# Loads of w3t units held three to ten units ahead of use, and queued behind the queries, in an attention and MoE kernel

## The chip, the core and the metric

The kernel runs on one core of a Trainium2 chip. Five engines matter: TensorE (PE, with its weight loads PEld), VectorE (DVE), ScalarE (ACT), GpSimd (POOL), and SyncE (SP), which here issues nearly all DMAs. Each engine works through its own list of instructions in a fixed order. The metric is device time in microseconds (us), the median of three runs.

## The reference

Three stages in float32, each fed by the one before. The weights are float64 in memory, q, k and v float32.

```python
def _attn_ref(q, k, v, g_q, g_k):            # (4, 12, 448, 64)
    q_n, k_n = rmsnorm(q, g_q), rmsnorm(k, g_k)
    scores = scale * np.matmul(q_n, k_n.transpose(0, 1, 3, 2))
    scores = scores - np.max(scores, axis=-1, keepdims=True)
    attn = np.exp(scores)
    attn = attn / (np.sum(attn, axis=-1, keepdims=True) + 1e-09)
    return np.matmul(attn, v)

def _moe_ref(x, w_in, w_out):                # 1792 x 768, d_ff 2048
    r = np.maximum(x @ w_in, 0.0)
    return (r * r) @ w_out

def _moe2_ref(x, w1, w2, w3, w_out):         # d_ff 1024
    return ((x @ w1) * (x @ w2) @ w3) @ w_out
```

## The kernel before

The four batches of 448 rows are worked one after the other. The 48 heads (batch b has the heads 12b to 12b + 11) run through a loop over `h`; beside the heads of one batch PE works on the dense layers ("fill") of the batch before. Beside the heads 0 to 12 there is no such batch yet, so the fill is a product of weights alone: `gen_w3o` multiplies w3 with the last w_out, 384 matmuls of 384 columns in 8 row blocks. Beside the heads 12 to 23 the fill is the two MoEs of batch 0 (`gen_moe(0)`), and so on. Below, batch 0 is the stretch of the heads 0 to 11 and batch 1 that of the heads 12 to 23.

**Units.** All weights come in pieces of 128 rows, numbered in the order of use. Units 0 to 31 are for `gen_w3o`: 0 and 5 are the two units of w3t's first row block, 1 to 4 and 6 to 17 are the last w_out, and 18 to 31 are two units of w3t for each of the row blocks 1 to 7. U0 = 32 is the first unit of w_in; units 32 to 119 are the weights of batch 0's MoEs, all of them float64 in memory. A float64 unit goes through these steps: a load into one of four buffers `raw64` (L319, on SP), Prelu on the high words (L333, ACT), the low words (L337 on ACT or L339 on POOL), a join into one of seven buffers `raw` (L346, DVE), a store of the float32 form for the later batches (L354, SP), a rounded high part (L144 `hl<-raw`, ACT) and the rest (L150 `hl<-raw,hl`, DVE or POOL). PE multiplies the parts in three matmuls (L411 to L413).

**A head.** Queries are loaded as `qt` (two buffers, L818) by `load_head`, called three heads ahead, and prepared by `head_prep` (L920 and L925). PE makes scores (L956, L957), DVE takes their negative maximum (L967) and scales it (L969), ACT takes the exponential (L991) into `p`, PE turns it (L1038, `pt`), ACT and DVE split it (`ptr`, `pte`), and PE multiplies with v (L1084, `kv`); DVE sums the two halves (L1092, `xf`). Norms are made for groups of four heads: a square (L862), a sum (L863), and a root by L832 to L839, with Ln and Exp on ACT (L837, L838). Scores have two PSUM banks, so a score waits for an exponential two scores back.

**What sets the order.** The code is traced in the order of the loop, and a scheduler then gives each engine its fixed list: it takes what it holds to be ready first, with the earlier traced one ahead, and it knows how many buffers there are. A load therefore stands early on SP when a `raw64` buffer is free, and its conversion steps stand early on ACT, DVE and POOL. `use(u)` is called by the fill for each unit, and it calls `advance(u)`: that traces the split of units up to u + 2 (u + 4 from U0 on), the joins up to two and the loads up to five (`LOAD64_AHEAD`) beyond that. `tc.issue_after(x)` orders what is traced under it behind instruction x on x's engine. It orders the issue alone; nothing waits until x is done.

Of the kernel before, what the change touches and what calls it, by code (L numbers as in the profile page):

```python
# [1 line left out]

# [9 lines left out]
U32 = mybir.dt.uint32  # L12
# [18 lines left out]
def attention_moe_kernel(  # L31
# [15 lines left out]
    nc = tc.nc  # L47
# [13 lines left out]
    NIC = w3t.shape[0] // 2  # L61
# [201 lines left out]
    def is64(i):  # L263
        return units[i][0].dtype != F32
# [46 lines left out]
    def load_next():  # L311
        i = pos["load"]
        src = units[i][0]
        while sum_of.get(i, -1) >= pos["sum"]:
            next(sums_left, None)
        n = src.shape[-1]
        if is64(i):
            t = t3.tile([128, 512, 2], U32, name="raw64", tag="raw64", bufs=4)
            nc.sync.dma_start(out=t[:, :n, :], in_=src.bitcast(U32).rearrange("p (n t) -> p n t", t=2))  # L319
        else:  # L320
            t = rawp.tile([128, 512], F32, name="raw", tag="raw")
            last["load"] = nc.sync.dma_start(out=t[:, :n], in_=src).ins
        raws[i] = t
        pos["load"] += 1
# [5 lines left out]
    def words(i):  # L330
        t, n = raws[i], units[i][0].shape[-1]
        hi = t[:, :n, 1].bitcast(F32)
        nc.scalar.activation(out=hi, in_=hi, func=AF.Prelu, scale=2.0**-112, alpha=-(2.0**32))  # L333
        low = t.rearrange("p n t -> p (n t)").bitcast(U16).rearrange("p (n t) -> p n t", t=4)[:, :n, 1]
        low_eng = LOW_ENG[i >= U0]
        if low_eng[i % len(low_eng)] == "a":
            nc.scalar.activation(out=t[:, :n, 0], in_=low, func=AF.Copy, scale=2.0**-13, bias=2.0**-14 - 0.5)  # L337
        else:
            nc.gpsimd.tensor_scalar(  # L339
                out=t[:, :n, 0], in0=low, scalar1=2.0**-13, scalar2=2.0**-14 - 0.5, op0=ALU.mult, op1=ALU.add  # L340
            )

    def join(i):
        t, n = raws[i], units[i][0].shape[-1]
        f = raws[i] = rawp.tile([128, 512], F32, name="raw", tag="raw")
        nc.vector.scalar_tensor_tensor(  # L346
            out=f[:, :n].bitcast(U32), in0=t[:, :n, 1], scalar=3, in1=t[:, :n, 0],
            op0=ALU.logical_shift_left, op1=ALU.bitwise_or,
        )
# [33 lines left out]
    def upto(what, i, step):  # L383
        while pos[what] <= min(i, NU - 1):
            step(pos[what])
            pos[what] += 1

    def advance(u):
        while pos["lo"] <= min(u + SPLIT_AHEAD + (2 if u >= U0 else 0), NU - 1):
            i = pos["lo"]  # L390
            for k in range(pos["load"], min(i + LOAD64_AHEAD, NU - 1) + 1):
                if is64(k):
                    load_next()
                elif k <= i + LOAD32_AHEAD and (k <= pos["join"] or not is64(k - 1)):
                    load_next()
                else:
                    break
            upto("store", min(i + JOIN_AHEAD, pos["join"]) - 1, lambda k: is64(k) and store(k))
            upto("word", i + WORD_AHEAD, lambda k: is64(k) and words(k))
            upto("join", i + JOIN_AHEAD, lambda k: is64(k) and join(k))  # L400
            upto("hi", i + HI_AHEAD, split_hi)
            upto("lo", i, split_lo)

    def use(u):
# [408 lines left out]
    def load_head(h):  # L813
        if not (0 <= h < NH):
            return
        b, hh = divmod(h, H)
        t = t2.tile([128, S], F32, name="qt", tag="qt")
        nc.sync.dma_start(out=t, in_=q_t[b, hh])  # L818
        qts[h] = t

    def load_v(h):
# [460 lines left out]
```

## Time and profile before

| | us |
|---|---|
| median of 3 runs | 1159.13 (1157.38 to 1160.3) |
| the profiled execution | 1156.4 |
| its span | 1154.6 |
| PE busy in the span | 1119.4 (97%) |
| DVE busy | 793.3 (69%) |
| ACT busy | 777.1 (67%) |
| POOL busy | 606.5 (53%) |

Busy shares over the span hide stages, so a table of stretches is read beside them: where PE is not full, what else is. A timeline then lists one engine's instructions with start and length; the bracket behind one is the idle time before it and the instruction that ended that. A group line sums instructions of one line and shape. PE's granted clock is a share of full speed, where 0.50 is 1.2 GHz and 1.00 is 2.4 GHz.

### The profile page before, as it was taken

To read this page: it belongs to the slowest core of one execution; us is meant where nothing else is said; L and a number is where in the kernel's file an instruction comes from. 1 tells how busy PE (TensorE), PEld (TensorE's weight loads), DVE (VectorE), ACT (ScalarE), POOL (GpSimd) and SP (SyncE) were. 2 spreads that over 40 slices of the span, in tenths; PEclk is the share of its full clock that TensorE was granted. 3 is DMA by queue.
4 is the path that set the end of the run, shared out by engine and by line. 5 is a ranking of instruction groups with operands and counts; after the bars stand their busy time and mean duration, and the time that the engine had idled before them with its cause. 6 is when DMAs were issued, how large, how long until landed. Compare 5 with 4: busy or idle time off the path is not lost.

```text
span 1154.6 us, 18788 instructions
## 1 busy us (share of the span) xinstructions
PE 1119.4 (97%) x5958; PEld 1015.1 (88%) x5958; DVE 793.3 (69%) x1363; ACT 777.1 (67%) x1768; POOL 606.5 (53%) x609
## 2 busy tenths in 40 slices
PE   7789999999999999999999999999999999999998
PEld 4678888988989899989999899999999899999997
DVE  7899889978988854564674755664544315887886
ACT  6888978978878866767776666776764445433352
POOL 3376433544435455956876775684855853011131
PEclk9899999999999999999999999999999999999999
DMA  7867758878988863575655657665546764243423
GB/s 250 268 194 227 221 156 262 309 273 282 323 274 273 299 197 128 166 220 164 221 178 163 207 184 244 187 200 165 183 155 205 224 191 122 72 134 104 130 84 122
DMA packets 130899, 229.74 MB, mean 199 GB/s; under 512 B 17472, under 2 KB 84544, under 8 KB 130800
## 3 DMA queue, kind: packets, MB, share of 16 engines
q1 hardware_dynamic: 129072, 225.79, 61.3%
q10 hardware_dynamic: 1728, 2.75, 0.7%
q8 instruction: 47, 0.77, 0.3%
q14 instruction: 52, 0.43, 0.1%
HBM read 162.53 MB, written 37.05 MB: 173 GB/s over the span
## 4 chain that ended last, share of the span: by engine, by line
PE 67%; ACT 10%; DVE 8%; DMA 8%; issue 3%; SPq 1%; POOL 1%; DVEq 0%; ACTq 0%; POOLq 0%
PE mm L411 16%; PE mm L412 16%; PE mm L413 16%; PE kv L1084 3%; PE pt L1038 3%; PE sc L956 2%; PE sc L957 2%; ACT p L991 2%; DMA raw<-w_in 2%; ACT raw L333 1%; DMA raw<-wo 1%; DVE nb L967 1%; DVE raw L346 1%; ACT hl L144 1%; DMA qn<-q_nat 1%
## 5 line engine op out<-in xcount | busy, mean ns | idle before, releaser
L150 POOL TENSOR_TENSOR hl<-raw,hl 128x384 fp32r<-128x384 f32 (+1 forms) x286 | 332.2, 1168 | 283.3 <-ACT hl L144 239.1
L144 ACT ACTIVATE hl<-raw 128x384 fp32r<-128x384 f32 (+1 forms) x405 | 227.6, 566 | 146.7 <-PE mm L413 41.1
L411 PE MATMUL mm<-x,hl 128*128 128x448 f32 (+1 forms) x640 | 237.9, 372 | 2.4 <-ACT x L144 2.4
L412 PE MATMUL mm<-x,hl 128*128 128x448 f32 (+1 forms) x640 | 234.2, 366 | 0.9 <-DVE x L150 0.8
L413 PE MATMUL mm<-x,hl 128*128 128x448 f32 (+1 forms) x640 | 233.4, 365 | 0.2 <-DVE hl L150 0.2
L411 PE MATMUL mm<-act,hl 128*128 128x448 f32 (+1 forms) x544 | 201.0, 369 | 1.9 <-ACT act L144 1.9
L412 PE MATMUL mm<-act,hl 128*128 128x448 f32 (+1 forms) x544 | 198.5, 365 | 3.0 <-DVE act L150 2.2
L413 PE MATMUL mm<-act,hl 128*128 128x448 f32 (+1 forms) x544 | 197.5, 363 | 0.0
L967 DVE TENSOR_REDUCE nb<-sc 128x1 f32<-128x448 f32 x168 | 102.7, 615 | 73.6 <-PE sc L957 72.2
L411 PEld LDWEIGHTS mm<-x,hl 128*128 128x128 f32 x640 | 120.9, 189 | 12.0 <-ACT x L144 3.5
L412 PEld LDWEIGHTS mm<-x,hl 128*128 128x128 f32 x640 | 121.0, 189 | 11.1 <-DVE x L150 2.6
L413 PEld LDWEIGHTS mm<-x,hl 128*128 128x128 f32 x640 | 120.8, 189 | 9.8 <-DVE hl L150 0.5
L991 ACT ACTIVATE p<-sc,nb,rr 128x448 f32<-128x448 f32 x168 | 121.5, 724 | 11.4 <-DVE nb L969 8.6
L150 DVE TENSOR_TENSOR ptr<-pt,ptr 128x512 fp32r<-128x512 f32 (+1 forms) x144 | 85.9, 617 | 51.3 <-ACT ptr L144 50.9
L412 PEld LDWEIGHTS mm<-act,hl 128*128 128x128 f32 x544 | 102.5, 189 | 11.8 <-DVE act L150 3.6
L411 PEld LDWEIGHTS mm<-act,hl 128*128 128x128 f32 x544 | 102.6, 189 | 9.2 <-ACT act L144 2.1
L413 PEld LDWEIGHTS mm<-act,hl 128*128 128x128 f32 x544 | 102.6, 189 | 7.7 <-DVE hl L150 0.3
L339 POOL TENSOR_SCALAR raw<-raw 128x384 uint32<-128x384 uint16 (+1 forms) x80 | 55.3, 691 | 93.6 <-DMA raw<-w_in 17.1
L346 DVE SCALAR_TENSOR_TENSOR raw<-raw 128x384 uint32<-128x384 uint32 (+1 forms) x120 | 88.5, 748 | 21.6 <-POOL raw L339 9.6
L956 PE MATMUL sc<-kt,qh 128*128 128x448 f32 (+1 forms) x192 | 73.6, 383 | 12.0 <-ACT p L991 6.3
L150 DVE TENSOR_TENSOR hl<-raw,hl 128x384 fp32r<-128x384 f32 (+1 forms) x119 | 79.7, 672 | 7.7 <-ACT hl L144 7.5
L333 ACT ACTIVATE raw<-raw 128x384 f32<-128x384 f32 (+1 forms) x120 | 71.5, 602 | 19.9 <-DMA raw<-w_in 10.4
(153 smaller groups left out, 2117.5 us busy)
## 6 DMA issues: line engine op xcount, KB each, us to landing
pw<-p SPq DMA_DIRECT2D x54, 448.0 KB
raw<-f_in SPq DMA_DIRECT2D x96, 192.0 KB
raw<-f_out SPq DMA_DIRECT2D x72, 256.0 KB
raw<-w_in SPq DMA_DIRECT2D x32, 384.0 KB
raw<-w_out SPq DMA_DIRECT2D x24, 512.0 KB
raw<-w SPq DMA_DIRECT2D x32, 384.0 KB
qt<-q_t SPq DMA_DIRECT2D x48, 224.0 KB
raw<-f SPq DMA_DIRECT2D x56, 192.0 KB
```

The lines of the kernel that those rows point to most:

```text
L144: return nc.scalar.activation(out=out, in_=in_, func=AF.Copy)
L150: return (nc.vector if eng == "v" else nc.gpsimd).tensor_tensor(out=out, in0=in0, in1=in1, op=op)
L333: nc.scalar.activation(out=hi, in_=hi, func=AF.Prelu, scale=2.0**-112, alpha=-(2.0**32))
L339: nc.gpsimd.tensor_scalar(out=t[:, :n, 0], in0=low, scalar1=2.0**-13, scalar2=2.0**-14 - 0.5, op0=ALU.mult, op1=ALU.add)
L346: nc.vector.scalar_tensor_tensor(out=f[:, :n].bitcast(U32), in0=t[:, :n, 1], scalar=3, in1=t[:, :n, 0], op0=ALU.logical_shift_left, op1=AL ...
L411: nc.tensor.matmul(ps, w[:, 0, wk, :], x[0], start=(i == 0), stop=False)
L412: nc.tensor.matmul(ps, w[:, 0, wk, :], x[1], start=False, stop=False)
L413: nc.tensor.matmul(ps, w[:, 1, wk, :], x[0], start=False, stop=(i == last))
L956: nc.tensor.matmul(out, d["qh"][:, at:at + m], d["kt"], start=True, stop=False)
L967: nc.vector.tensor_reduce(out=nb[:, j:j + 1], in_=o[j], axis=AX.X, op=ALU.max, negate=True)
L991: nc.scalar.activation(out=p, in_=o[j], func=AF.Exp, scale=d["rq"][:, c:c + 1], bias=nb[:, j:j + 1], accum_out=sm[:, c:c + 1],)
L1038: nc.tensor.transpose(to[:kn, j * 128:(j + 1) * 128], d["p"][c][:, k0:k0 + kn], one)
```

## The change

Two things are changed in how loads of float64 units are traced. `load_limit(u)` limits which unit may be loaded by the time unit u is used. Until unit 18 (row block 1) is used that is unit 19; in the row blocks 1 to 7 it is u + 3, 3, 4, 5, 6, 8 and 10; from unit 32 on there is no limit but the old one. As before, a load is at most five units beyond the unit that is split. Joins, Prelu steps and splits go no further than the loads. And each load of the units 20 to 43 (`SLOW`) is traced under `tc.issue_after(last["q"])`, so that it is issued behind the load of queries that was traced last.

```diff
         if is64(i):
             t = t3.tile([128, 512, 2], U32, name="raw64", tag="raw64", bufs=4)
-            nc.sync.dma_start(out=t[:, :n, :], in_=src.bitcast(U32).rearrange("p (n t) -> p n t", t=2))
+            with tc.issue_after(last["q"]) if SLOW[0] <= i < SLOW[-1] else nullcontext():
+                nc.sync.dma_start(out=t[:, :n, :], in_=src.bitcast(U32).rearrange("p (n t) -> p n t", t=2))
...
+    SLOW = (U0 - NIC * 2 + 4, U0 + 12)
+    ROWS = (3, 3, 3, 4, 5, 6, 8, 10)
+
+    def load_limit(u):
+
+        if u >= U0:
+            return NU - 1
+        row = (u - (U0 - NIC * 2)) // 2
+        if row < 1:
+            return SLOW[0] - 1
+        return u + ROWS[row]
+
     def advance(u):
         while pos["lo"] <= min(u + SPLIT_AHEAD + (2 if u >= U0 else 0), NU - 1):
             i = pos["lo"]
-            for k in range(pos["load"], min(i + LOAD64_AHEAD, NU - 1) + 1):
+            for k in range(pos["load"], min(i + LOAD64_AHEAD, load_limit(u), NU - 1) + 1):
...
-            upto("word", i + WORD_AHEAD, lambda k: is64(k) and words(k))
-            upto("join", i + JOIN_AHEAD, lambda k: is64(k) and join(k))
-            upto("hi", i + HI_AHEAD, split_hi)
+            got = pos["load"] - 1
+            upto("word", min(i + WORD_AHEAD, got), lambda k: is64(k) and words(k))
+            upto("join", min(i + JOIN_AHEAD, got), lambda k: is64(k) and join(k))
+            upto("hi", min(i + HI_AHEAD, got), split_hi)
             upto("lo", i, split_lo)
...
-        nc.sync.dma_start(out=t, in_=q_t[b, hh])
+        last["q"] = nc.sync.dma_start(out=t, in_=q_t[b, hh]).ins
```

The scheduler makes new lists from this. They differ from the middle of the first batch (head 2) to the heads 24 to 26 and are the same behind that. Three places follow; line numbers behind L387 are 14 higher in the changed kernel, and L319 is L320 there.

The first is SP's list in row block 1, from the load of unit 18 (`raw64_500`) to the queries of head 5 (`qt`), before and then now:

```order
L319 DMA raw64_500<-w3t 128x1024
L319 DMA raw64_537<-w3t 128x1024
L319 DMA raw64_551<-w3t 128x1024
L319 DMA raw64_582<-w3t 128x1024
L319 DMA raw64_596<-w3t 128x1024
L319 DMA raw64_615<-w3t 128x1024
L319 DMA raw64_650<-w3t 128x1024
L439 DMA w3o_99<-osb_664 128x3x128
L319 DMA raw64_668<-w3t 128x1024
L1005 DMA rsd_700<-rt_698 7x32 x4
L818 DMA qt_742<-q_t 128x448
```

```order
L320 DMA raw64_500<-w3t 128x1024
L320 DMA raw64_537<-w3t 128x1024
L320 DMA raw64_646<-w3t 128x1024
L320 DMA raw64_648<-w3t 128x1024
L821 DMA kn_1020<-k_nat 112x1024
L453 DMA w3o_99<-osb_642 128x3x128
L1019 DMA rsd_686<-rt_684 7x32 x4
L840 DMA v_864<-v_in 128x256
L822 DMA qn_1019<-q_nat 128x896
L832 DMA qt_728<-q_t 128x448
L320 DMA raw64_742<-w3t 128x1024
```

Of the eight loads of w3t ahead of the queries four are left. The keys and natural queries of group 2 (`kn`, `qn`) and a load of v stand ahead of them instead, and unit 22 behind them.

The second is ACT's list at the same time, from the square of group 1's keys (`qn<-kn`) to the exponentials of head 3 (`p,sm`), or to the second step of the norm where that now comes later:

```order
L862 ACTIVATE qn<-kn 112x1024
L333 ACTIVATE raw_596<-raw_596 128x512
L144 ACTIVATE hl<-raw 128x512
L333 ACTIVATE raw_615<-raw_615 128x512
L337 ACTIVATE raw_615<-raw_615 128x512
L920 ACTIVATE qh<-qt,gg 128x448
L333 ACTIVATE raw_650<-raw_650 128x512
L837 ACTIVATE nt<-nt 128x32
L144 ACTIVATE hl<-raw 128x512
L838 ACTIVATE nt<-nt 128x32
L991 ACTIVATE p,sm<-sc,nb,rr 128x448 x2
```

```order
L876 ACTIVATE qn<-kn 112x1024
L144 ACTIVATE hl<-raw 128x512
L934 ACTIVATE qh<-qt,gg 128x448
L1005 ACTIVATE p,sm<-sc,nb,rr 128x448 x2
L144 ACTIVATE ptr<-pt 128x384
L851 ACTIVATE nt<-nt 128x32
L144 ACTIVATE ptr<-pt 128x384
L852 ACTIVATE nt<-nt 128x32
```

The Prelu steps of three units and a low-word step are gone from here, and the exponentials now stand ahead of the norm's Ln and Exp (L837 and L838, now L851 and L852).

The third is SP's list at the start of batch 1, from a store of exponentials (`pw`) and the queries of head 16 on:

```order
L1015 DMA pw_2314<-p_2297 128x896
L818 DMA qt_2340<-q_t 128x448
L319 DMA raw64_2575<-w_in 128x768
L354 DMA f_in_114<-raw_2540 128x384
L319 DMA raw64_2594<-w_out 128x1024
L1015 DMA pw_2487<-p_2407 128x896
L354 DMA f_in_114<-raw_2580 128x384
L826 DMA v_2657<-v_in 128x256
L319 DMA raw64_2669<-w_out 128x1024
L354 DMA f_in_114<-raw_2599 128x384
L319 DMA raw64_2688<-w_out 128x1024
```

```order
L1029 DMA pw_2314<-p_2297 128x896
L832 DMA qt_2340<-q_t 128x448
L320 DMA raw64_2355<-w_in 128x768
L320 DMA raw64_2365<-w_in 128x768
L320 DMA raw64_2375<-w_in 128x768
L320 DMA raw64_2394<-w_in 128x768
L320 DMA raw64_2432<-w_in 128x768
L355 DMA f_in_114<-raw_2399 128x384
L320 DMA raw64_2462<-w_in 128x768
L355 DMA f_in_114<-raw_2437 128x384
L1029 DMA pw_2487<-p_2407 128x896
```

Ahead of these queries SP had 47 loads of units and now has 39, so units 39 to 43 follow in a row behind them. Ahead of the queries of head 18 both lists have 57 loads. On DVE, 43 joins stood ahead of the first maximum of head 12 and 39 do now; on ACT, 46 Prelu steps stood ahead of its first exponential and 39 do now; on POOL, 28 low-word steps stood ahead of the keys of head 12 (L904) and 23 do now. From there to head 24 ACT and DVE convert a unit directly ahead of its split, where they had some two to six units in stock before.

## Rows read from the trace of the kernel before

**Rows 1.** the page, part 1: busy time and share of the span of each engine.
```profile
PE 1119.4 (97%) x5958; PEld 1015.1 (88%) x5958; DVE 793.3 (69%) x1363; ACT 777.1 (67%) x1768; POOL 606.5 (53%) x609
```

**Rows 2.** busy time in stretches: length, engines (instructions), granted clock, DMA share, GB/s.
```profile
46.00:62.00 16.00, 14.81 (x73) 12.58 (x72) 15.77 (x28) 13.01 (x27) 8.48 (x8) 0.90 0.70 229
62.00:80.00 18.00, 15.10 (x88) 12.98 (x88) 16.60 (x27) 16.31 (x38) 13.92 (x17) 1.00 0.73 220
80.00:180.00 100.00, 93.96 (x556) 85.40 (x556) 90.51 (x180) 87.47 (x205) 46.67 (x56) 1.00 0.66 200
180.00:300.00 120.00, 117.59 (x631) 106.95 (x630) 105.50 (x177) 101.51 (x240) 57.52 (x63) 0.99 0.86 288
300.00:450.00 150.00, 147.14 (x784) 134.56 (x784) 108.97 (x193) 110.65 (x262) 70.21 (x73) 1.00 0.76 253
450.00:1154.00 704.00, 697.52 (x3677) 641.20 (x3675) 420.69 (x678) 414.67 (x926) 393.25 (x365) 1.00 0.53 167
274.60:278.00 3.40, 3.38 (x14) 2.90 (x13) 3.40 (x7) 3.40 (x8) 2.23 (x3) 0.50 1.01 264
```

**Rows 3.** SP's timeline: start, us, line, tiles, count.
```profile
41.43 12.50 SPq L319 DMA_DIRECT2D raw<-w3t  x7
...
62.30 0.36 SPq L818 DMA_DIRECT2D qt<-q_t  x1
...
91.52 0.43 SPq L319 DMA_DIRECT2D raw<-w_in  x1
...
179.45 0.53 SPq L818 DMA_DIRECT2D qt<-q_t  x1
180.03 1.00 SPq L319 DMA_DIRECT2D raw<-w_in  x1
```

**Rows 4.** ACT's timeline near 62 us; in brackets the idle before, and who ended it.
```profile
61.71 0.23 ACT L837 ACTIVATE nt<-nt 128x32 f32<-128x32 f32 x1 [2.33 <-DVE nt L836]
...
62.61 0.72 ACT L991 ACTIVATE p<-sc,nb,rr 128x448 f32<-128x448 f32 x1
```

**Rows 5.** DVE's timeline, 59 to 62 us.
```profile
59.09 1.21 DVE L832 TENSOR_SCALAR rr<-ss 128x32 int32<-128x32 int32 x1
...
60.45 1.13 DVE L346 SCALAR_TENSOR_TENSOR raw<-raw 128x512 uint32<-128x512 uint32 x1
61.50 0.18 DVE L836 TENSOR_TENSOR nt<-nt,ss 128x32 f32<-128x32 f32 x1
```

**Rows 6.** PE's timeline at three places.
```profile
63.47 0.47 PE L956 MATMUL sc<-kt,qh 128*128 128x448 f32 x1 [2.06 <-ACT p L991]
...
73.24 0.51 PE L941 MATMUL kv<-ident_r,khl 112*128 112x112 f32 x4 [1.38 <-DVE xf L1092]
...
179.44 0.37 PE L411 MATMUL mm<-x,hl 128*128 128x448 f32 x1
```

**Rows 7.** groups by shape, 46 to 180 us: count, busy us, mean ns, idle before.
```profile
L956 PE MATMUL sc<-kt,qh 128*128 128x448 f32 x40 | 16.6, 415 | 6.4 <-ACT p L991 6.1 <-ACT kt L144 0.3
...
L333 ACT ACTIVATE raw<-raw 128x512 f32<-128x512 f32 x14 | 9.5, 675 | 0.2 <-DMA raw<-w3t 0.2
L333 ACT ACTIVATE raw<-raw 128x384 f32<-128x384 f32 x16 | 9.0, 560 | 1.3 <-DMA raw<-w_in 1.2
...
L346 DVE SCALAR_TENSOR_TENSOR raw<-raw 128x384 uint32<-128x384 uint32 x14 | 8.3, 594 | 0.7 <-POOL hl L150 0.6
```

**Rows 8.** POOL's timeline near 59 us.
```profile
58.98 1.28 POOL L150 TENSOR_TENSOR hl<-raw,hl 128x512 fp32r<-128x512 f32 x1
```

**Rows 9.** ACT's timeline at two waits for w_in loads.
```profile
244.38 0.55 ACT L333 ACTIVATE raw<-raw 128x384 f32<-128x384 f32 x1 [3.23 <-DMA raw<-w_in]
...
266.16 0.57 ACT L333 ACTIVATE raw<-raw 128x384 f32<-128x384 f32 x1 [2.66 <-DMA raw<-w_in]
```

**Rows 10.** PE's timeline at 274 us.
```profile
274.19 1.02 PE L1038 MATMUL pt<-ident_r,pw 128*128 128x128 f32 x6 [1.86 <-DVE ptr L150]
```

**Rows 11.** groups by shape, 180 to 450 us.
```profile
L411 PE MATMUL mm<-x,hl 128*128 128x448 f32 x195 | 73.3, 376 | 0.0
```

More of the change, by code (lines that the diff above doesn't have):

```diff
@@ L1 @@
-from contextlib import ExitStack
+from contextlib import ExitStack, nullcontext
 import concourse.bass as bass
```

## The prediction

> **What bounds the kernel now.** I read the busy shares first, then a table of stretches, then the three engines that feed TensorE in the stretch where it waits, and last the queue of loads. Over the span PE is busy 97% [rows 1], so the end moves only if PE waits less, or runs less at half clock. The table of stretches shows where it waits: 1.19 us of 16 from 46 to 62, 2.90 of 18 from 62 to 80, 6.04 of 100 from 80 to 180, then 2.41 of 120, 2.86 of 150, and 6.48 in the last 704 us [rows 2]. From 46 to 180 (the heads of batch 0) DVE is the fullest other engine, 15.77 of 16, 16.60 of 18 and 90.51 of 100, with ACT close behind at 87.47 of 100 [rows 2]. So batch 0 is run by DVE and ACT together, and from 180 on PE sets the time. Whatever batch 0 gains goes to the end if later stretches don't add a wait.
>
> In batch 0 the reader is to see one pattern. SP issues seven w3t loads in a row from 41.43 for 12.50 us, and the next queries go out at 62.30 only [rows 3]. As those units land, their conversion steps become ready and stand in the engines' fixed order ahead of attention work. On DVE a join (L346) begins at 60.45, takes 1.13 us, and the norm's step L836 follows at 61.50 [rows 5]. ACT's Ln (L837) waits 2.33 us for that, and the exponential stands behind the Ln, at 62.61 [rows 4]. PE waits 2.06 us for it, until 63.47 [rows 6]. Much of this was not wanted yet: SP issues even the first w_in load at 91.52 [rows 3], and PE's first matmul on a w_in unit (the first of 448 columns on weights) is at 179.44 [rows 6].
>
> **The change, part by part.** *Loads held back.* No instruction is added or taken away; the edges are of issue order alone. They hold loads, and with them Prelu, low word, join and split. By the two orders, DVE has 43 joins ahead of head 12's first maximum before and 39 now; ACT has 46 Prelu steps ahead of head 12's first exponential and 39 now. The rest is made up by head 24.
>
> *The stall at 61.* ACT now has two Prelu steps, not five, between the copy of `osb` and the exponential of head 3, and the Ln stands behind the exponential. Three Prelu steps of 512 columns at 0.675 us [rows 7] and the wait of 2.33 [rows 4] are 4.4 us, more than PE's wait of 2.06 [rows 6]. I take the whole 2.06 as gone. What is late next there is PE's wait of 1.38 at 73.24, behind DVE's sum for `xf` [rows 6]; I leave that to the next term. Ends: 0 and 2.06.
>
> *The rest of batch 0.* From 62 to 180 PE waits 2.90 + 6.04 = 8.94 us [rows 2]; 1.47 of it is the tail of the first wait (63.47 less 62.00), so 7.47 can go. Most waits here are of one kind: from 46 to 180 scores wait 6.1 us for ACT's exponential [rows 7]. DVE loses four joins of w_in units at 0.594 us, 2.4 us; ACT loses seven Prelu steps at 0.560, 3.9 us [rows 7]. I take the 2.4, since DVE is the fuller engine and the maxima and sums that release the exponential are on it. Ends: 0 (the freed slots are filled again) and 3.9.
>
> *Queries.* Eight loads of w3t stood between the first of the loads at 41.43 and the queries of head 5; four do now, but the keys and natural queries of group 2 and a load of v come in between. The queries should go out a few us ahead of 62.30 [rows 3]. That is part of the first term; I add nothing.
>
> *What waits behind the new order.* On SP, each load of units 20 to 43 is queued behind the queries of its time, and these wait until a buffer is free. Behind the load stand v, stores of `w3o` and the row sums. In batch 0 this costs nothing: the limit keeps three to ten units in hand.
>
> *The hand-over at 180.* SP has 47 loads ahead of the queries of head 16 before, and 39 now. Those queries go out at 179.45 and the next load right after, at 180.03 [rows 3]. So w_in units 39 to 46 are now fetched after that point, when PE has begun to eat them (179.44) [rows 6]. Seven units (32 to 38) are still in hand, and both orders have 57 loads ahead of the queries of head 18. Before, PE waited 0.0 us for any `hl` in batch 1 at the row of its first matmul [rows 11], since units were ready early. I take 0 here. Ends: from the gain and the loss of the rivals below.
>
> *A rule against it.* The row shows loads issued 88 us ahead of use (91.52 to 179.44) [rows 3, 6], and the steps that they release in the way of attention [rows 4, 5]. The Trainium skill, page "DMA: Bandwidth & Descriptors", section "Rules for kernel authors", advises to issue a DMA early and wait for it late. By that rule the change gives cover away and gains nothing, and the sum would be zero or a loss, as in the third rival; by the rows it gains. The trace so far agrees with the rows in batch 0, and no row shows the case where the cover is thin.
>
> *A second one.* DVE's step L832 on 32 columns took 1.21 us at 59.09 [rows 5], beside a POOL subtraction of 1.28 us that began at 58.98 [rows 8]. The Trainium skill, page "SBUF — State Buffer", section "SBUF: two separate sides", says that the two engines lock a shared port pair for a whole instruction. By it, five POOL low-word steps fewer up to head 12 would free DVE of some blocking too. If that is one stretched step like this one, about 1 us, the sum would be 5.5 and not 4.5 (an estimate from that page's rule and these two rows). I leave it out.
>
> **Sum.** 2.06 + 2.4 = 4.5 us. The profiled execution took 1156.4 us for a span of 1154.6; the median of the runs shown is 1159.13, so I put the change on that: 1159.13 - 4.5 = 1154.6. A measurement of this kernel tells about 0.3% from no change, which is 3.5 us: faster means below 1155.6, slower above 1162.6.
>
> **Rivals.**
> *No change to speak of.* The slots that the conversions leave are filled by work that was ready anyway: the new DVE order has the sums and norm of group 2 earlier, between the heads 4 and 6. DVE stays full and PE's wait of 2.06 comes back at another score. For it: DVE's 90.51 of 100 [rows 2] leaves little room to move. Against it: four joins really leave batch 0. Also in this case is that limits don't bind because four raw buffers already did; the order speaks against that. About 1 us of gain, 1158.
>
> *A larger gain.* In batch 1 ACT waited 3.23 us at 244.38 and 2.66 at 266.16 for w_in loads [rows 9], and PE then 1.86 at 274.19 [rows 10], after which the clock stood at 0.50 for 3.4 us [rows 2], which costs half of that, 1.7. The new order puts Prelu about four units later against attention, so the load may have landed. If these waits go, PE gets back 1.86 + 1.7, and of the 5.27 us that it waits from 180 to 450 [rows 2] perhaps 1 more: 4.5 us. With the forecast's 4.5 the gain is 9, 1150.
>
> *Slower: units arrive late in batch 1.* Now ACT has Prelu and split of a unit close together, and few units in stock, from 180 on. If loads land late there, ACT stands still in its fixed order, the exponential behind it too, and PE stops as at 274.19: 1.86 of waiting [rows 10] and 1.7 of half clock [rows 2], 3.6 us each time. From two such stops on (7.2 us) the gain of 4.5 is eaten; with three it is 10.7 - 4.5 = 6.2 us slower, 1165. For it: ACT did wait three microseconds in such places [rows 9]. Against it: PE never waited for `hl` there [rows 11], and the loads per unit of time are the same.
>
> **How the numbers follow.** Forecast (gain 2 to 6, 1153 to 1157) 0.47; no change 0.22; larger gain 0.18; slower 0.13. Faster by over 0.3%: three quarters of the forecast and the larger gain, 0.35 + 0.18 = 0.53. Within: the rest of the forecast and no change, 0.34. Slower: 0.13. For eight in ten the range leaves out the outer part of the larger gain and most of the slower case: 1149 to 1162. The forecast's own range is 1153 to 1157.
>
> **What would show it.** In the profile after: (1) no wait of PE near 61 for an exponential, and the queries of head 5 out before 60; (2) PE through batch 0 some 4.5 us sooner, so that its first 448-column matmul on weights stands near 175 and not at 179.44; (3) joins and Prelu of w_in fewer before that point; (4) from 180 to 450 PE's waits still near 5 us. If (2) holds and the time does not move, the hand-over took it back; if (2) fails, the freed slots were filled again.

## The result and the profile after

The change makes the kernel slower: 1171.53 us (median of 6 runs, 1168.97 to 1179.74), beside 1158.26 us for the kernel before on the same chip (6 runs). The ratio is 1.013, with an interval of 1.010 to 1.016. The forecast was 1154.6 in a range of 1149 to 1162. The profiled execution took 1171.3 us for a span of 1169.5, 14.9 us more than before. From the ends of the heads (the last `kv` matmul of each) in the two traces:

| us | before | after | difference |
|---|---|---|---|
| end of head 1 (see below) | 68.9 | 66.3 | -2.6 |
| end of head 2 | 79.4 | 78.9 | -0.4 |
| end of head 11 (batch 0 ends) | 178.8 | 181.0 | +2.2 |
| heads 12 to 23 (batch 1) | 268.4 | 280.9 | +12.5 |
| from head 23 to the end | 707.4 | 707.6 | +0.2 |

The first row doesn't compare like with like. PE's order is another one there: up to the last `kv` matmul of head 1 it has done 16 instructions fewer than before, 14 of them fill matmuls of `w3o`, which now come behind. At the end of head 2 it has done the same work in both kernels.

Lines behind the new functions have moved: the load is L320 now, Prelu L334, low words L338 and L340, the join L347, queries L832, scores L970, the exponential L1005, `pt` L1052, the three matmuls L425 to L427.

The table of stretches after, against [rows 2] (length, then busy time of PE, PEld, DVE, ACT and POOL, granted clock, DMA share, GB/s), and a last row with a stretch of half clock:

```profile
46.00:62.00 16.00, 13.97 (x70) 11.72 (x68) 14.67 (x29) 13.23 (x30) 6.00 (x6) 0.94 0.58 173
62.00:80.00 18.00, 16.53 (x98) 14.58 (x98) 16.25 (x29) 16.27 (x36) 12.76 (x16) 1.00 0.66 208
80.00:180.00 100.00, 91.64 (x544) 83.12 (x543) 84.17 (x170) 82.42 (x193) 42.95 (x53) 1.00 0.56 167
180.00:300.00 120.00, 113.88 (x614) 103.25 (x613) 98.64 (x172) 102.21 (x237) 54.64 (x63) 1.00 0.89 295
300.00:450.00 150.00, 141.60 (x741) 127.24 (x740) 110.89 (x200) 114.42 (x261) 68.38 (x72) 0.98 0.85 266
450.00:1169.00 719.00, 712.61 (x3748) 654.84 (x3746) 424.20 (x682) 421.91 (x944) 400.04 (x372) 1.00 0.53 166
331.40:334.80 3.40, 3.02 (x13) 2.70 (x14) 2.80 (x6) 2.23 (x6) 0.00 (x0) 0.50 0.70 233
```

From 80 to 180 DVE and ACT have 5 to 6 us less to do than before, and PE still does less. From 180 to 450 PE waits 6.12 + 8.40 = 14.52 us; before it was 5.27. The same view from the end of head 11 to that of head 23, before and then after:

```profile
178.80:447.20 268.40, 263.14 (x1405) 240.01 (x1404) 213.38 (x368) 210.70 (x496) 127.04 (x135) 0.99 0.81 271
...
181.00:461.90 280.90, 266.38 (x1405) 240.39 (x1404) 209.53 (x372) 220.97 (x507) 128.49 (x140) 0.99 0.85 273
```

The same 1405 matmuls. PE waits 14.52 and not 5.26, so 9.3 us are waiting. Its half clock lasts 6.8 us there (from 331.4 and from 379.2, beside stops of 3.43 and 1.81 us) and 3.4 before, which costs 1.7 more. That makes 11.0 of the 12.5 us. The other 1.5 us are busy time of PE, and no row shows what made it longer.

What PE waits for from 180 to 460, before and then after (what is waited for, us in total, times, longest):

```profile
PE sc L956 <- ACT kt L144: 2.9, 3, 1.3
PE pt L1038 <- DVE ptr L150: 1.9, 1, 1.9
PE pt L1038 <- DMA pw<-p: 0.4, 1, 0.4
...
PE pt L1052 <- DVE ptr L150: 13.0, 8, 3.4
PE pt L1052 <- DMA pw<-p: 1.5, 2, 1.1
```

Not one of these waits is for a weight: as in [rows 11], PE doesn't stop for any `hl`. It stops for `pt`, whose buffers come free when DVE has split the last ones. What holds DVE is seen in the groups of 180 to 450 (busy and mean, then idle time before them and what ended it), ACT and DVE of before, then of after:

```profile
L144 ACT ACTIVATE hl<-raw 128x384 fp32r<-128x384 f32 (+1 forms) x100 | 56.4, 569 | 3.2 <-PE mm L413 3.0
L333 ACT ACTIVATE raw<-raw 128x384 f32<-128x384 f32 (+1 forms) x73 | 43.5, 607 | 15.4 <-DMA raw<-w_in 9.2 <-DMA raw<-w 3.6 <-DMA raw<-w_out 2.5
L346 DVE SCALAR_TENSOR_TENSOR raw<-raw 128x384 uint32<-128x384 uint32 (+1 forms) x75 | 58.3, 792 | 17.8 <-POOL raw L339 7.8 <-ACT raw L337 4.4 <-ACT raw L333 2.7
...
L144 ACT ACTIVATE hl<-raw 128x384 fp32r<-128x384 f32 (+1 forms) x96 | 53.9, 562 | 28.2 <-DVE raw L347 26.8 <-DMA raw<-w3o 0.7
L334 ACT ACTIVATE raw<-raw 128x384 f32<-128x384 f32 (+1 forms) x81 | 47.1, 582 | 0.4 <-DMA raw<-w_in 0.4
L347 DVE SCALAR_TENSOR_TENSOR raw<-raw 128x384 uint32<-128x384 uint32 (+1 forms) x81 | 55.6, 688 | 28.3 <-POOL raw L340 11.3 <-ACT raw L338 5.3 <-DMA f_out<-raw 2.6
```

Before, ACT stood in front of loads (15.4 us) and never in front of a join. After, it is the other way round: 0.4 us for loads, 26.8 us in front of splits whose join isn't done. One such place, from the timelines of POOL, DVE, ACT, DVE and PE:

```profile
228.65 1.16 POOL L150 TENSOR_TENSOR x<-xf,x 128x448 fp32r<-128x448 f32 x1 [5.11 <-ACT x L144]
229.90 0.64 POOL L340 TENSOR_SCALAR raw<-raw 128x512 uint32<-128x512 uint16 x1
...
230.57 0.69 DVE L347 SCALAR_TENSOR_TENSOR raw<-raw 128x512 uint32<-128x512 uint32 x1 [2.38 <-DMA f_out<-raw]
...
231.35 0.63 ACT L144 ACTIVATE hl<-raw 128x512 fp32r<-128x512 f32 x1 [1.70 <-DVE raw L347]
233.88 0.63 ACT L144 ACTIVATE hl<-raw 128x512 fp32r<-128x512 f32 x1 [0.32 <-DVE raw L347]
234.42 1.06 ACT L144 ACTIVATE ptr<-pt 128x512 fp32r<-128x512 f32 x2
...
236.31 1.27 DVE L150 TENSOR_TENSOR ptr<-pt,ptr 128x512 fp32r<-128x512 f32 x2
...
237.05 0.53 PE L1052 MATMUL pt<-ident_r,pw 128*128 128x128 f32 x4 [2.72 <-DVE ptr L150]
```

A low word on POOL ends at 230.54, DVE's join has stood 2.38 us (the row names a store, but the low word ends in the same instant), ACT's split 1.70, and behind them in the fixed lists stand the two halves of `ptr` for which PE stops 2.72. The chain join, split, `ptr` runs with nothing in hand.

How much is in hand can be counted in the fixed lists: joins ahead of the split at the first exponential of each head. From head 14 to 22 the kernel before has 5, 3, 4, 5, 4, 3, 4, 3, 4 (3.9 on average), the changed one 0 or -1. Below this is called the **stock**.

### The profile page after: what moved, and what is told of

Its sections match the earlier page's. It is cut to its first block, busy times and chain, and to the rows that moved or that the text cites. A ratio compares the mean times of both kernels' runs of the same rounds, so it can differ in the third digit from the quotient of the medians.

```text
span 1169.5 us, 18764 instructions
## 1 busy us (share of the span) xinstructions
PE 1126.1 (96%) x5958; PEld 1018.4 (87%) x5958; DVE 783.6 (67%) x1363; ACT 783.4 (67%) x1768; POOL 601.3 (51%) x609
## 5 line engine op out<-in xcount | busy, mean ns | idle before, releaser
L425 PE MATMUL mm<-x,hl 128*128 128x448 f32 (+1 forms) x640 | 238.4, 372 | 1.0 <-ACT x L144 1.0
L427 PE MATMUL mm<-x,hl 128*128 128x448 f32 (+1 forms) x640 | 233.7, 365 | 0.2 <-DVE hl L150 0.2
L425 PE MATMUL mm<-act,hl 128*128 128x448 f32 (+1 forms) x544 | 202.1, 372 | 1.9 <-ACT act L144 1.9
L427 PE MATMUL mm<-act,hl 128*128 128x448 f32 (+1 forms) x544 | 198.4, 365 | 0.0
L425 PEld LDWEIGHTS mm<-x,hl 128*128 128x128 f32 x640 | 120.8, 189 | 10.7 <-ACT x L144 2.1
L427 PEld LDWEIGHTS mm<-x,hl 128*128 128x128 f32 x640 | 120.9, 189 | 9.8 <-DVE hl L150 0.5
L1005 ACT ACTIVATE p<-sc,nb,rr 128x448 f32<-128x448 f32 x168 | 121.1, 722 | 12.0 <-DVE nb L983 8.9
L425 PEld LDWEIGHTS mm<-act,hl 128*128 128x128 f32 x544 | 102.9, 189 | 9.2 <-ACT act L144 2.1
L427 PEld LDWEIGHTS mm<-act,hl 128*128 128x128 f32 x544 | 102.9, 189 | 7.8 <-POOL hl L150 0.4
L347 DVE SCALAR_TENSOR_TENSOR raw<-raw 128x384 uint32<-128x384 uint32 (+1 forms) x120 | 81.2, 679 | 35.8 <-POOL raw L340 17.8
L970 PE MATMUL sc<-kt,qh 128*128 128x448 f32 (+1 forms) x192 | 73.7, 384 | 11.1 <-ACT p L1005 7.8
L340 POOL TENSOR_SCALAR raw<-raw 128x384 uint32<-128x384 uint16 (+1 forms) x80 | 55.5, 693 | 50.7 <-DMA raw<-w3t 18.7
L144 ACT ACTIVATE ptr<-pt 128x512 fp32r<-128x512 f32 (+1 forms) x144 | 73.6, 540 | 9.3 <-PE pt L1052 8.7
```

The costliest lines, as they stand in the source:

```text
L144: return nc.scalar.activation(out=out, in_=in_, func=AF.Copy)
L340: nc.gpsimd.tensor_scalar(out=t[:, :n, 0], in0=low, scalar1=2.0**-13, scalar2=2.0**-14 - 0.5, op0=ALU.mult, op1=ALU.add)
L347: nc.vector.scalar_tensor_tensor(out=f[:, :n].bitcast(U32), in0=t[:, :n, 1], scalar=3, in1=t[:, :n, 0], op0=ALU.logical_shift_left, op1=AL ...
L425: nc.tensor.matmul(ps, w[:, 0, wk, :], x[0], start=(i == 0), stop=False)
L427: nc.tensor.matmul(ps, w[:, 1, wk, :], x[0], start=False, stop=(i == last))
L970: nc.tensor.matmul(out, d["qh"][:, at:at + m], d["kt"], start=True, stop=False)
```

## Experiments

The theory: of the w_in units, 32 to 42 were joined in batch 0, beside attention (43 joins ahead of head 12, now 39), and that stock was carried through all of batch 1. The change holds them back, PE eats from 181.63 on what is just being converted, and nothing builds the stock up again. The rivals: the loads that come late in batch 0; the row limits; half clock alone.

All of them in one table: "batch 0" is the end of head 0 to that of head 11, "batch 1" that of head 11 to that of head 23, both from one trace, the ratio is against the kernel before. In e5, e6 and e7 18 more of PE's instructions come before the end of head 0, so their batch 0 is less work than that of the others; their head 11 ends at 182.9, 177.4 and 184.5 us (178.8 before).

| kernel | stock | batch 0 | batch 1 | ratio (interval) |
|---|---|---|---|---|
| before; again (e8) | 3.9 | 129.3; 128.8 | 268.4; 267.6 | 1 |
| changed; again (e15) | -0.2 | 131.3; 133.2 | 280.9; 281.6 | 1.013 (1.010 to 1.016) |
| e1 one edge at 39; again (e16) | 0 | 129.2; 127.9 | 280.1; 278.8 | 1.009 (1.006 to 1.013) |
| e2 limits, edges 20 to 31 | 3.1 | 133.6 | 269.3 | 1.007 (1.004 to 1.009) |
| e3 limits alone | 3.7 | 129.6 | 272.2 | 1.005 (1.002 to 1.007) |
| e4 edges alone; again (e18) | -0.2 | 126.0; 126.4 | 281.0; 281.0 | 1.008 (1.005 to 1.011) |
| e5 e1 with look-aheads | 4.8 | 128.2 | 276.9 | 1.014 (1.011 to 1.017) |
| e6 changed with look-aheads | 2.0 | 124.5 | 276.2 | 1.008 (1.005 to 1.011) |
| e7 before with look-aheads | 4.4 | 129.2 | 271.5 | 1.011 (1.008 to 1.014) |
| e9 e1, split later | 1.2 | 128.2 | 273.0 | 1.004 (1.003 to 1.006) |
| e10 changed, split later | 1.1 | 132.7 | 277.6 | 1.013 (1.011 to 1.015) |
| e11 one edge at 43 | 2.3 | 129.1 | 273.1 | 1.005 (1.003 to 1.006) |
| e12 one edge at 36 | 2.2 | 131.6 | 273.9 | 1.007 (1.005 to 1.010) |
| e13 edges 20 to 33 | 3.9 | 129.0 | 269.0 | 1.000 (0.998 to 1.002) |
| e14 edges 20 to 31 | 3.7 | 134.2 | 273.4 | 1.008 (1.005 to 1.011) |
| e17 edges 20 to 35 | 3.4 | 130.3 | 278.0 | 1.008 (1.006 to 1.011) |

### One edge, and each half of the change

e1 is the kernel before with one edge:

```diff
+            with tc.issue_after(last["q"]) if i == U0 + 7 else nullcontext():
                 nc.sync.dma_start(out=t[:, :n, :], in_=src.bitcast(U32).rearrange("p (n t) -> p n t", t=2))
...
-        nc.sync.dma_start(out=t, in_=q_t[b, hh])
+        last["q"] = nc.sync.dma_start(out=t, in_=q_t[b, hh]).ins
```

> The kernel before with one single edge: the load of w_in unit 39 is queued behind the load of the latest queries. Loads before it (all of w3t and units 32 to 38) are as in the kernel before, so the joins stand one to five units ahead of the split up to head 8 as before, and with no unit in stock from head 13 to 23, as in the changed kernel. Stock theory (units converted in advance are lost at the hand-over, so the chain Prelu, low word, join, split runs just in time on engines that take their work in order): batch 0 as before, batch 1 (from the end of head 11 to that of head 23) 280 us and not 268, PE's waits from 180 to 450 some 14 us and not 5, the whole 1.010 to 1.013 of the kernel before. Rival, late loads in batch 0 (the w3t loads behind queries make attention wait): nothing of that is in here, so 1.000. Rival, half clock: two more such stretches at most, 3.4 us, 1.003.

e2 is the changed kernel with edges up to unit 31 only, e3 without edges, e4 without limits. The three edits, one after the other:

```diff
-            with tc.issue_after(last["q"]) if SLOW[0] <= i < SLOW[-1] else nullcontext():
+            with tc.issue_after(last["q"]) if SLOW[0] <= i < U0 else nullcontext():
...
-            with tc.issue_after(last["q"]) if SLOW[0] <= i < SLOW[-1] else nullcontext():
+            with nullcontext():
...
-        if u >= U0:
+        if u >= 0:
```

> The changed kernel with its queue edges on the w3t units 20 to 31 alone; the limits by row block stay, the w_in units 32 to 43 go without an edge. In the fixed order batch 0 is that of the changed kernel up to head 9, and the joins are four units ahead again from head 12 on, as before. Stock theory: head 1 ends 2.5 us sooner as in the changed kernel, batch 1 takes 268 us as before, the whole 0.997 to 1.001. Rival, late loads in batch 0: most of the loss stays, 1.008 to 1.012. Rival, the fixed order of batch 1 differs for another reason: 1.005 or more.

> The changed kernel with the limits by row block and no queue edge at all. The stock is that of the kernel before from head 6 on. Stock theory: batch 1 268 us, the whole 0.998 to 1.001; the wait of PE at 61 us partly there again. Rival, that the limits cost: 1.005 or more.

> The kernel before with the queue edges of units 20 to 43 and without the limits by row block. The joins have no stock from head 13 on, as in the changed kernel. Stock theory: batch 1 280 us, the whole 1.010 to 1.013. Rival, that the limits are the cause: 1.000.

One edge gives batch 1 nearly its whole loss: 280.1 us (11.7 of the 12.5 us), with batch 0 as before. That settles the place: not the w3t loads, not the limits. e4 has the loss (281.0) and e2 doesn't (269.3). e3 is at 272.2, above what was expected. The groups of ACT from 180 to 450 in e1 show the same sign as after:

```profile
L144 ACT ACTIVATE hl<-raw 128x384 fp32r<-128x384 f32 (+1 forms) x97 | 54.2, 562 | 27.2 <-DVE raw L347 22.7 <-PE mm L414 1.8 <-POOL hl L150 1.1
L334 ACT ACTIVATE raw<-raw 128x384 f32<-128x384 f32 (+1 forms) x81 | 47.4, 585 | 0.4 <-DMA raw<-w_in 0.2
```

For the whole, e1 and e4 (1.009 and 1.008) fell just short of the expected 1.010, and e2 and e3 came out worse than expected; e2 lost 4 to 5 us in batch 0, e3 has a stop of its own in batch 1 (below), and both profiled executions lost 4 us in their last part, which is no work of the change (last section). Half clock alone is no cause: e1 had 10.2 us of it in batch 1, which costs 5.1 less 1.7 of before, out of 11.7. It also wanders from one execution to the next: 3.4 and 0 us in the two of the kernel before, 6.8 and 10.2 in those of the changed one.

### Is it ACT's standing in front of the join?

e9 is e1 with one more order on ACT, e10 the changed kernel with it. Loads and joins keep their places; only the split stands further behind its join (so the stock, counted at the splits, reads 1.2 and 1.1 without a unit more being converted).

```diff
+        pre[i] = nc.scalar.activation(out=hi, in_=hi, func=AF.Prelu, scale=2.0**-112, alpha=-(2.0**32)).ins
...
+        with tc.issue_after(pre[i + 2]) if U0 + 7 <= i and i + 2 in pre else nullcontext():
+            copy_on("a", t[:, 0, :n], raws[i][:, :n])
```

> The one-edge kernel (unit 39 behind the latest queries) with one more order on ACT: from unit 39 on, the high split of a unit stands behind the Prelu of the unit two further on. Loads and joins keep the places that they have with the one edge (no unit in stock, by joins against queries and maxima); only ACT no longer asks for a join right after it is issued. In the one-edge kernel ACT stood still 22.7 us in batch 1 in front of 27 splits for a join, in the kernel before not at all. Theory A (ACT's stops in its fixed order are the loss): these stops fall under 8 us, batch 1 takes 268 to 273 us and not 280, the whole 0.998 to 1.004. Theory B (the loss is DVE's own: its join stands in front of the low word, and behind it the low part of ptr for which PE waits): batch 1 stays at 277 to 283 us, 1.009 or more.

> The changed kernel with the same order on ACT (high split behind the Prelu of two units on, from unit 39). Theory A: batch 1 268 to 273 us and not 281, the whole 0.999 to 1.005. Theory B: 278 to 283 us, 1.010 or more.

The group row of the splits in e9, 180 to 450, and what PE waits for from 180 to 460:

```profile
L144 ACT ACTIVATE hl<-raw 128x384 fp32r<-128x384 f32 (+1 forms) x99 | 54.7, 557 | 3.3 <-PE mm L417 3.3
...
PE pt L1042 <- DVE ptr L150: 5.2, 6, 1.7
PE mm L417 <- POOL hl L150: 1.7, 2, 0.9
PE mm L417 <- DVE hl L150: 0.7, 1, 0.7
```

And the first of PE's waits in e10, in the same stretch:

```profile
PE pt L1055 <- DVE ptr L150: 6.2, 4, 2.9
```

ACT's 22.7 us in front of joins are gone, and 7.1 of the 11.7 us in batch 1 come back (273.0), about half of it as waits of PE (12.6 us in e1, 8.9 now) and half as busy time (no stretch of half clock is left). Up to the end of head 19 all of it is back: heads 12 to 19 take 172.7 us, 173.0 before and 180.5 in e1. Then PE waits for weights (POOL's and DVE's low parts of `hl`), since the split was only put off: no unit more is in hand than in e1. So in the one-edge kernel theory A holds for the larger part; that the rest is the missing stock itself is argued, not shown. In e10 ACT's stops in front of joins fall from 26.8 to 0.9 us as well, and yet only 3.3 of 12.5 us come back (277.6): my expectation there is missed. In the changed kernel itself ACT's stops are thus shown to be about a quarter of the loss. PE's waits for `ptr` fall from 13.0 to 6.2 us, the joins on DVE still stand 20.9 us (28.3 after). Part of theory B stays.

### How much stock is needed

e11 and e12 move the one edge to the units 43 and 36. e5, e6 and e7 widen the look-aheads in e1, in the changed kernel and in the kernel before:

```diff
-    JOIN_AHEAD = 2
-    WORD_AHEAD = 3
-    LOAD64_AHEAD = 5
+    JOIN_AHEAD = 5
+    WORD_AHEAD = 6
+    LOAD64_AHEAD = 8
```

> The one edge on unit 43 in place of 39: four units more are loaded ahead of the hand-over. The joins stand one to four units ahead of the split from head 14 to 22 (2.3 on average; 3.9 before, 0 with the edge on 39). Stock theory: batch 1 270 to 274 us, the whole 1.000 to 1.005. Rival, the edge costs by itself wherever it is: 278 us or more.

> The one edge on unit 36, an earlier one: the queries behind which it is queued go out before the end of batch 0, and the loads catch up (two to three units in stock on average from head 14 to 22). Units 36 to 38 are held back too, and yet the stock is larger than with the edge on 39. Stock theory: batch 1 270 to 274 us; batch 0 0 to 2 us shorter than before, since joins leave heads 8 to 10; the whole 0.999 to 1.004. Rival, the edge costs by itself, or holding back more units costs more: 280 us or more.

> The kernel with one edge (w_in unit 39 behind the latest queries), with the stock given back in another way: the look-aheads are 5 for the join, 6 for the word steps and 8 for the load, where they were 2, 3 and 5. The edge stays; in the fixed order the joins stand four to seven units ahead of the split from head 14 to 22, where the one edge alone had none. Stock theory: batch 1 (end of head 11 to end of head 23) 267 to 271 us as before and not 280, no waits of PE for pt behind a join on DVE, the whole 0.997 to 1.003. Rival, the edge costs by itself (its load comes late, or the queries do): 280 us, 1.008 or more.

> The changed kernel with the same look-aheads (5, 6 and 8). All limits and edges stay; the joins stand two to three units ahead from head 14 to 20 and one to two after, half of the stock of the kernel before. Stock theory: batch 1 271 to 276 us, so the change's loss there is halved; batch 0 as in the changed kernel, 181 to 184 us; the whole 1.003 to 1.008. Rival, the edge costs by itself: 280 us, 1.010 to 1.013.

> The kernel before with the look-aheads 5, 6 and 8: about one unit more in stock in batch 1 (four to six). It tells whether the look-aheads do anything by themselves. Stock theory: the kernel before has enough in stock, so batch 1 266 to 269 us and the whole 0.997 to 1.002. Rival, look-aheads alone gain several us: 0.995 or less.

With 2.0 to 2.3 in stock batch 1 takes 273 to 276 us, between 268 and 280, about as expected (e6, at 276.2, is just outside); that holding back more units (e12) costs less than holding back fewer (e1) speaks against the edge itself as the cause. But what PE waits for isn't the same in the three: `ptr` for 9.8 us in e6, and for only 0.4 and 0.5 in e11 and e12, where `pw` (a copy of `p`, moved by SP) takes 9.4 and 5.2. So a stock of two units can take the waits of the chain away, and another wait takes their place. e12 missed in batch 0 (131.6 us, 2.3 more than before) and in the whole (1.007), e6 in batch 0, which ends at 177.4 and not at 181 to 184. e5 and e7 are clear misses. e5 has more stock than before and takes 276.9 us; e7 takes 271.5, and both end head 11 later than before, by 4.1 and 5.7 us. What PE waits for in e5 from 180 to 460, and one such place there, from the timelines of ACT, SP, DVE and SP:

```profile
PE pt L1039 <- DMA pw<-p: 9.4, 5, 3.4
...
239.64 0.73 ACT L992 ACTIVATE p<-sc,nb,rr 128x448 f32<-128x448 f32 x1
...
237.81 0.47 SPq L355 DMA_DIRECT2D f_in<-raw  x1
244.82 1.30 SPq L1006 DMA_DIRECT2D rsd<-rt  x4
...
244.58 0.21 DVE L1003 STREAM_TRANSPOSE rt<-rs 128x32 f32<-128x32 f32 x1
...
248.15 0.47 SPq L1016 DMA_DIRECT2D pw<-p  x1
```

No split stands in front of a join here. `p` was done at 240.4, but its copy `pw` stands on SP behind four transfers of row sums, two loads and two stores, and SP waits from 238.3 to 244.8 for the `rt` of those row sums, which DVE makes late in its list. PE waits 9.4 us for `pw` in e11 too and 7.3 in e7; before it was 0.4. So a stock alone isn't enough: what is moved on one list meets another queue.

### Batch 0, and a version between the two

e13, e14 and e17 are e4 with the edges ending at unit 33, 31 and 35 (`SLOW[0] <= i < U0 + 2`, `U0`, `U0 + 4`); e8, e15, e16 and e18 are second executions.

> The kernel before itself, a second profiled execution, to see how far the ends of heads and the last 200 us wander from one execution to the next with the same order of instructions. If they wander little, batch 0 ends at 178 to 180 and batch 1 takes 267 to 270 us; head 1 may end 1 to 3 us later or earlier, since the one edge moved it by 2.4 us with the same order there.

> The kernel before with queue edges on units 20 to 33 and no limits: in the fixed order the joins of heads 6 to 10 stand later by one to four units, and from head 11 on the stock is that of the kernel before. If edges without limits shorten batch 0 (they did with edges up to 43: head 0 to head 11 took 126.0 us, before 129.3 and 128.8) and the stock keeps batch 1: batch 0 126 to 127 us, batch 1 267 to 270 us, the whole 0.996 to 0.999, so better than both kernels. Rival, the 3 us in batch 0 came from the w_in joins that went to batch 1, which are in batch 0 again here: 129 us, 0.999 to 1.002. Rival, as with limits and w3t edges: the loads crowd at heads 9 to 11 and batch 0 takes 131 us or more, 1.002 to 1.006.

> The same with edges on the w3t units 20 to 31 alone. Less is moved: joins of heads 6 to 9 by one or two units. Batch 0 127 to 129 us, batch 1 267 to 270 us, the whole 0.997 to 1.000; by the crowding rival 1.002 or more.

> The changed kernel itself, a second profiled execution: whether its batch 0 (131.3 us from the end of head 0 to that of head 11, two us more than before) and its batch 1 (280.9) come again. If both are its own: 131 to 133 and 280 to 282 us; the last 900 matmuls at 30.4 us per 150 as in its first execution, unless that pace changes by chance.

> The one-edge kernel itself, a second execution. Its last 900 matmuls took 31.0 us per 150, with 30.4 in the kernel before, in the same order of instructions. If that is a matter of the execution, it may be 30.4 now and the end 4 us sooner; if it belongs to the kernel, 31.0 again. Batch 1 280 us again.

> Queue edges on units 20 to 35, no limits: between the edges to 33 (batch 0 129.0, batch 1 269.0 us, the time of the kernel before) and the edges to 43 (126.0 and 281.0). In the fixed order the joins of heads 7 to 11 stand later, the stock is back to within one unit of before from head 11 on. If the joins that leave batch 0 carry its 3 us: 127 to 128 us there and 268 to 271 in batch 1, 0.997 to 1.000. If, as with the edges to 31, ACT's Prelu stands in front of a load near 250 us with the exponential behind it, batch 1 takes 273 us and the whole is 1.003 or more.

> The kernel with the edges of units 20 to 43 and no limits, a second execution. Head 0 to head 11 took 126.0 us, 3 us under the kernel before; executions of one kernel have wandered by 0.5 to 1.9 us there. 125 to 127.5 if it is its own, 128 to 129 if it was chance. Batch 1 280 to 282 us again.

Second executions agree within 2 us in either batch. Edges on the units 20 to 43 without limits shorten batch 0 by 3 us (126.0 and 126.4); with the limits the same edges lengthen it by 2 to 4 (131.3, 133.2, and 132.7 in e10); limits alone do nothing (129.6). The two together bring a wait that neither has alone: with three units in hand, a load behind the queries lands just as it is wanted. From 46 to 180 us ACT stands 2.9 us in front of loads of w3t in the changed kernel (0.2 before), and at most 0.1 in e3 and e4. The row of those Prelu steps after, against [rows 7]:

```profile
L334 ACT ACTIVATE raw<-raw 128x512 f32<-128x512 f32 x14 | 9.3, 667 | 2.9 <-DMA raw<-w3t 2.9
```

That this wait is all that limits and edges cost in batch 0 is not shown: e6 has 3.7 us of it, and its head 11 ends sooner than before. One place of it, from the timelines after, SP, ACT and PE:

```profile
83.19 0.36 SPq L832 DMA_DIRECT2D qt<-q_t  x1
83.59 0.44 SPq L320 DMA_DIRECT2D raw<-w3t  x1
...
89.21 0.69 ACT L334 ACTIVATE raw<-raw 128x512 f32<-128x512 f32 x1 [1.37 <-DMA raw<-w3t]
89.92 0.54 ACT L144 ACTIVATE vt<-kv 64x448 f32<-64x448 f32 x1
90.48 0.72 ACT L1005 ACTIVATE p<-sc,nb,rr 128x448 f32<-128x448 f32 x1
...
91.35 0.47 PE L970 MATMUL sc<-kt,qh 128*128 128x448 f32 x1 [1.57 <-ACT p L1005]
```

No version beat the kernel before, though e13, e14 and e17 were expected to be equal or better. e13 is equal to it (1.000), with its stock; its batch 0 (129.0) is that of its first rival, by which the 3 us that e4 gains there belong to the w_in joins that e4 puts off. e14 and e17, with nearly the same stock, lost 5 to 10 us in batch 1, and e14 lost 5 in batch 0 as well, where its granted clock was 0.96 (1.00 after). SP and ACT in e14 show why:

```profile
246.72 1.30 SPq L1019 DMA_DIRECT2D rsd<-rt  x4
...
250.25 0.37 SPq L320 DMA_DIRECT2D raw<-w_in  x1
...
254.29 0.55 ACT L334 ACTIVATE raw<-raw 128x384 f32<-128x384 f32 x1 [5.56 <-DMA raw<-w_in]
...
261.86 0.74 PE L970 MATMUL sc<-kt,qh 128*128 128x448 f32 x1 [4.39 <-ACT kt L144]
```

Queries, v and four transfers of row sums stand ahead of the load on SP, ACT waits 5.56 us for it with exponentials behind it, and PE stops 4.39. Here the conversion stands too early in ACT's list. It is the kind of wait of [rows 9], which in the kernel before takes 3.23 and 2.66 us at two places. e3 (4.97 us) and e17 (5.12) have it too.

## Why the prediction was wrong

**The step that failed** is the hand-over at 180, taken as 0: it is 12.5 us of the 14.9. (The forecast was -4.5, so it is off by 19.4 us: 12.5 here, 6.7 in batch 0, which ended 2.2 us later and not 4.5 sooner, and 0.2 behind.) The argument was that PE waited 0.0 for any `hl` [rows 11]. It still waits for none. The units are on time; what they lost is their stock, and a unit that is on time with no stock makes ACT stand in front of its join (26.8 us) and DVE in front of its low word, with the `ptr` that PE needs behind both. PE's waits for `ptr` rose from 1.9 to 13.0 us. That the held-back w_in units are the cause is shown from both sides: one edge on unit 39 gives 280.1 us, and without edges on w_in (e2) batch 1 takes 269.3. I looked at who waits for a weight, and not at what stands behind the wait.

**The stall at 61**: the wait went as forecast, the gain of 2.06 us didn't come. The queries go out ahead of 60 (59.65), and there is no wait for an exponential near 61. But the 2.6 us by which head 1 ends sooner are work put off: the 14 fill matmuls of the table's first row, which follow each other every 0.17 us or so near 58, make 2.4 of it. PE waits 2.03 us from 46 to 62 and 1.47 from 62 to 80, together 3.5 where it was 4.1 [rows 2]: other waits took its place, as the first rival had it, such as 1.29 us at 62.54 for a norm's step on DVE. By the end of head 2, with the same work done, 0.4 us are left (1.6 between the second executions). From the timelines after, SP and PE, against [rows 3, 6]:

```profile
59.65 0.38 SPq L832 DMA_DIRECT2D qt<-q_t  x1
...
62.54 0.52 PE L1052 MATMUL pt<-ident,p 128*128 128x128 f32 x3 [1.29 <-DVE rr L853]
...
181.63 0.37 PE L425 MATMUL mm<-x,hl 128*128 128x448 f32 x1
```

**The rest of batch 0**, 2.4 us for four joins fewer, didn't come: the first 448-column matmul on weights is at 181.63, not at 175. The joins did leave (39 ahead of head 12). The runs give no one price for them: the same four joins fewer gave 0.6 us in e1 (129.2, 127.9, and 128.2 in e9, against 129.3 and 128.8) and about 3 in e4, with edges on w3t. Nor were the freed slots filled again, as the first rival said: DVE was busy 84.17 us from 80 to 180, 90.51 before, and PE still did less. So the reason for the term, that DVE is the fuller engine, didn't hold; a less busy DVE did not let PE wait less. And limits with edges cost 5 to 7 us against edges alone (131.3 and 133.2, 126.0 and 126.4), for which there was no term. I had written that the limits keep three to ten units in hand and that a load behind the queries costs nothing; ACT's waits for w3t rose from 0.2 to 2.9 us.

**The rival "slower"** had the place and the cause half right: few units in stock, engines in fixed order, PE stopped and half clock behind. It had ACT wait for loads, where it hardly waits for them any more in batch 1 (0.4 us), and three stops, where PE stopped nine times for 0.7 us or more. Its price of 3.6 us a stop was too high: two of the nine came with 3.4 us of half clock, and the one of 2.72 us at 237.05 did not. It gave 1165 and had 0.13; by [rows 9] it deserved more, since those rows showed ACT standing still for three microseconds in the same stretch.

**The rules.** The advice in the Trainium skill, page "DMA: Bandwidth & Descriptors", section "Rules for kernel authors", to issue a DMA early and wait late, is borne out, though in batch 1 by another way than a late transfer: there ACT's waits for loads fell from 15.4 to 0.4 us, and only in batch 0 those for w3t grew. Nearer to the cause is the page "PSUM — Partial Sum Buffer", section "Engine vs sequencer instructions", where the queues of ScalarE, VectorE and GpSimd are strict first in, first out; the 26.8 us agree.

**Open.** Why e10 gets back only 3.3 us where e9 gets 7.1 wasn't separated, nor how much of theory B is in it. So the loss in batch 1 is shown to come from the w_in units held back, while its division between ACT's and DVE's stops is not. What makes limits and edges together lengthen batch 0 is open as well.

## What to carry over

In this kernel, where engines run fixed lists, work that was done long before its use wasn't idle stock: it was the distance that kept a producer's wait out of the consumer's list, and the loop, running at the pace of its use, never earned it back. Before holding a load back, count in the lists how many units lie between each step and the next at the place where the use begins, and look at what stands behind each step, not only at whether its result is on time. Then check the other side: a step put far ahead of its load stops the engine as well.

## What was not expected of the hardware

**The pace of the last part.** The last 900 matmuls or so run without a gap in all traces, in the same order. In some executions 150 of them take 30.4 us, in others 31.0, about 4 us in the end. The kernel before had 30.4 in both of its profiled executions and e1 31.0 in both, but the changed kernel had 30.4 in its first execution and 31.0 in its second (1178.59 us, the end 4.4 us later from head 35 on). The stretch from 980 to 1150 in the first and then in the second (columns as in the table of stretches; 840 and 824 matmuls):

```profile
980.00:1150.00 170.00, 170.00 (x840) 157.58 (x839) 135.82 (x229) 74.91 (x145) 32.58 (x28) 1.00 0.36 109
...
980.00:1150.00 170.00, 170.00 (x824) 154.40 (x823) 131.69 (x224) 73.68 (x142) 32.03 (x27) 1.00 0.36 105
```

The granted clock reads 1.00 in both. No run shows the cause; it is why the ends of heads were compared here and not the spans.

**Joins beside POOL.** From 180 to 450 the 24 joins of the kernel before that ran beside no POOL instruction took 0.60 us on average, the 51 others 0.88; after, 43 took 0.59 and 38 took 0.80. The Trainium skill, page "SBUF — State Buffer", section "SBUF: two separate sides", has GpSimd and a DVE instruction with two inputs in SBUF, as a join is, shut each other out of a shared pair of ports when the GpSimd one reads SBUF; the traces agree. With fewer joins beside POOL they were cheaper after (55.6 us for 81, and 58.3 for 75 before), and the time didn't follow.
